# Priorities for the last exponentials and the merge, readings loaded one ahead, and the last store in halves, in an interleaved attention kernel

## The chip, the cores and the metric

The kernel runs on one core of a Trainium2 chip. A core has five engines that run side by side, each with its own queue of instructions: TensorE (PE in the profile, with its weight loads as PEld) multiplies matrices into PSUM; VectorE (DVE) and ScalarE (ACT) work on tiles element by element; GpSimd (POOL) works on tiles too; SyncE (SP) here only starts transfers. Transfers are also started from ScalarE's and GpSimd's queues. Engines wait for one another by semaphores, and an instruction that waits holds up all that stand behind it on its engine. The metric is the device time of one execution in microseconds (us).

## The reference

Four layers run one after the other on 2048 rows of 640 numbers, in the order A, B, A, B. Each adds its result to its input, after a layer norm without weights. Both have 32 heads of 20 numbers.

```python
def _A_ref(x, wqkv, wo):            # linear attention, not causal
    phi = lambda t: where(t > 0, t + 1, exp(t)) + 1e-6
    pq, pk = phi(q), phi(k)
    kv = einsum("bhsd,bhse->bhde", pk, v);  z = einsum("bhsd->bhd", pk)
    num = einsum("bhqd,bhde->bhqe", pq, kv)
    den = einsum("bhqd,bhd->bhq", pq, z)[..., None] + 1e-6
    return merge_heads(num / den) @ wo

def _B_ref(x, wq, wk, wv, wo, beta):  # 4 segments of 512 rows, with a memory M, z
    for s in range(4):
        p = softmax(qs @ ks.T * scale + causal_mask);  a_dot = p @ vs
        a_mem = (phi(qs) @ M) / (phi(qs) @ z + 1e-6)
        o = g * a_mem + (1 - g) * a_dot
        M, z = M + phi(ks).T @ vs, z + phi(ks).sum()
    return merge_heads(o) @ wo

x = A_x
for layer in (_A_ref, _B_ref, _A_ref, _B_ref):
    x = x + layer(layernorm(x), ...)
```

## The kernel before

The rows are cut into four segments of 512, and each segment into four tiles of 128 rows. Matrices that need more than 16 bits are kept as an upper half and a lower half (two f16 numbers whose sum is the value): ScalarE writes the upper half, VectorE subtracts it from the source and writes the lower half, and TensorE multiplies three of the four pairs. So a lower half on VectorE always stands behind an upper half on ScalarE. PSUM is used as a ring of eight banks, `ps`.

The order of TensorE's instructions is that in which the program issues them (`MANUAL = ("PE",)`). For the other engines a scheduler sets the order, by priority (by default the place in the program) and by what it thinks is ready; `high_priority(offset=...)` raises or lowers what is issued under it, and `issue_after(x)` keeps instructions behind x on their engine or by a wait.

**Layer A, first pass** (`g_first`). A tile x of 128 rows is loaded (L342, on SP's queue). `moments` takes its mean and variance on VectorE (L350 to L354) and the power -1/2 on GpSimd (L355); `shift` multiplies mean and scale into the bias `nb` (L360); `normed` writes the normalised tile xh on ScalarE (L386). `turn` transposes xh on TensorE (L331; three 128x128 blocks into one bank, two into another) and writes xT, the upper half on ScalarE (L335) and the lower on VectorE (L336). `proj_n` projects (L414). phi of keys and queries is an exponential and a relu on ScalarE (L428, L430) and a VectorE step (L431); the upper halves of the keys are L566 on ScalarE and the lower ones L553 on VectorE. `parts` copies xh for the product of keys and rows (L497 on ScalarE). `opening` weaves the first segment's norms, turns and weights together; there TensorE's order has the five transposes of tile 2 and the first three of tile 3 in one piece. Weights arrive as f32 in `stage` (L241), are scaled, split (L271 upper, L272 lower) and stored (L277, SP's queue).

**Merge.** At the end of the pass `merge` folds the sums G (L612 adds to them) and the values' and output's weights into one matrix wm per layer. For each half n it scales five parts (L669, L671), splits them (L673 upper, L674 lower), and TensorE multiplies them with w_Av (L692). The kt parts follow (L698, L701, L702), the products with the output weights (L722, L728), and the split of wm (L731 upper, L732 lower). In the first layer the last weight, w_Bo, is split at the same time: five L272 of 128x640 on VectorE. `open_b` then sets a tile `one` (L841, a memset on VectorE) and copies it into the key stacks (L844, six small transfers on SP's queue).

**Layer A, second pass** (`a_head`, `a_second`). `p_load` reads phi of the queries back from DRAM (L754, SP's queue); `p_read` scales it (L764), sums it per head (L768), takes the reciprocal (L769, L770) and multiplies (L771 on GpSimd). The result is turned (L331, L335, L336 into oT), multiplied by wm (L414) and added to the input xo (L342 for the load, L493 for the addition). `tail` turns the last two tiles of the segment for layer B, while TensorE has begun layer B's values.

**Layer B.** `b_project` projects values, which ScalarE spreads out with a column of ones per head (`v_half`, L445), then queries and keys (L399, split in L850 and L851, phi in L438 to L441). `attention` runs over 32 groups of four heads per layer. A group's stacks qs and ks are loaded; TensorE computes scores (L1015) of which VectorE takes row maxima (L1021, two instructions each, and L1030 and L1031 to split them); the maxima are turned (L1039) and stored as extra rows of qs; then the scores come again with the maximum in them (L1056), ScalarE takes exponentials (L1060), GpSimd zeroes what lies above the diagonal (L1067), and TensorE multiplies with the values (L1083). `EXPS` names the exponentials in five steps k. Steps 0 to 3 run in the group's own time slot, step 4 in the next one. `b_out` multiplies with w_Bo and adds the input (L490 and L491, or L493 at the very end, where the segment has `ends`), and stores the tile of 128x640 (L982, on ScalarE's queue).

## Time and profile before

| | us |
|---|---|
| median of 3 runs | 1696.86 (1695.87 to 1697.17) |
| the profiled execution's own time | 1699.81 |
| its span in the profile | 1698.1 |
| PE busy | 1641.3 |
| DVE busy | 1264.6 |
| ACT busy | 995.1 |
| POOL busy | 505.9 |

In rows of the waits, an engine and line stand before the arrow and the line that released it behind, then us in total, number of waits and the longest. In rows of a timeline stand the start, the duration, the engine, the line, the operation, `out<-in`, and in brackets the idle time ahead of it with its releaser; neighbouring equal instructions are one row (`x13`). In rows of stretches stand the stretch, its length, the busy us of PE, PEld, DVE, ACT and POOL with counts, the granted clock of TensorE (1.00 is full), and the share and GB/s of the DMA engines. Line numbers are those of the kernel before; those of the kernel after are a few higher.

### The profile page before, as it was taken

What the parts mean: (1) busy time and instruction counts of PE and PEld (TensorE: products, weight loads), DVE (VectorE), ACT (ScalarE), POOL (GpSimd) and SP (SyncE); (2) the same over time, 40 slices, a digit from 0 to 9 for tenths busy, and PEclk for the clock granted to TensorE, in tenths of its full rate; (3) what the DMA queues carried; (4) which work ended last, traced back from release to release, by engine and by line L of the source; (5) the groups of instructions that cost most, each with busy time, mean ns of one, the idle gap of its engine ahead of it and who ended that gap; (6) DMA issues with size and microseconds to landing.
All of it is one profiled execution on the core that took longest, in us unless ns stands there. A gap on an engine that the chain in (4) does not pass through costs nothing. (4 is left out here: it accounts for less than half of the span.)

```text
span 1698.1 us, 37894 instructions
## 1 busy us (share of the span) xinstructions
PE 1641.3 (97%) x13818; PEld 1021.1 (60%) x13818; DVE 1264.6 (74%) x4015; ACT 995.1 (59%) x1888; POOL 505.9 (30%) x1046
## 2 busy tenths in 40 slices
PE   8999989999999999999999999999999999999998
PEld 6767767564565566556556777766546546645555
DVE  7788886497887787768864566938888888777773
ACT  6666543357657656667665554433675675666763
POOL 4442232022223423433342211210322332232542
PEclk9999999999999999999999999999999999999999
DMA  6415563422312331461211303533232333323422
GB/s 219 156 57 184 214 246 119 148 87 78 114 68 70 127 111 60 134 206 51 80 45 48 108 32 124 191 97 119 76 111 82 104 100 102 106 83 111 148 87 95
DMA packets 110371, 190.99 MB, mean 112 GB/s; under 512 B 14172, under 2 KB 69596, under 8 KB 107624
## 3 DMA queue, kind: packets, MB, share of 16 engines
q1 hardware_dynamic: 97704, 142.68, 26.0%
q0 software_dynamic: 3264, 24.91, 4.1%
q10 hardware_dynamic: 9216, 20.98, 3.2%
q8 instruction: 109, 1.79, 0.4%
q14 instruction: 78, 0.64, 0.1%
HBM read 109.32 MB, written 78.64 MB: 111 GB/s over the span
## 5 line engine op out<-in xcount | busy, mean ns | idle before, releaser
L1021 DVE CUSTOM_DVE_ANT_0 ps<-ps,maskw 128x512 f32<-128x512 f32 (+3 forms) x1024 | 472.1, 521 | 43.8 <-PE ps L1015 41.6
L1060 ACT ACTIVATE pe<-ps,lsc 128x512 f32<-128x512 f32 x640 | 396.7, 696 | 84.5 <-PE ps L1056 82.7
L1067 POOL TENSOR_SCALAR_AFFINE_SELECT pe<-pe 128x256 f32<-128x256 f32 (+1 forms) x640 | 233.3, 372 | 387.6 <-ACT pe L1060 379.6
L414 PEld LDWEIGHTS <-xT 128*128 128x128 f16 x2880 | 280.3, 98 | 112.5 <-issue 6.2
L414 PEld LDWEIGHTS <-oT 128*128 128x128 f16 x1920 | 185.5, 98 | 82.3 <-issue 6.8
L1083 PE MATMUL ps<-pe,v 128*32 128x512 f32 (+3 forms) x2048 | 166.4, 436 | 7.8 <-POOL pe L1067 2.2
L414 PE MATMUL ps<-w_Bo,oT 128*128 128x320 f16 x960 | 143.5, 302 | 3.6 <-ACT oT L335 2.0
L1021 DVE DVE_READ_ACCUMULATOR2_ANT mg<- 128x1 f32 x1024 | 145.2, 142 | 0.0
L590 PE MATMUL ps<-pk,xs 128*128 128x321 f16 (+1 forms) x960 | 138.4, 302 | 4.2 <-DVE pk L553 2.0
L399 PE MATMUL ps<-xT,w_Bq 128*128 128x512 f16 x600 | 140.9, 380 | 1.3 <-ACT pe L1060 0.8
L414 PE MATMUL ps<-wm,oT 128*128 128x320 f16 x960 | 141.0, 299 | 0.5
L414 PE MATMUL ps<-w_Ak,xT 128*128 128x320 f16 x960 | 139.0, 300 | 2.3 <-DVE xT L336 1.6
L414 PE MATMUL ps<-w_Bv,xT 128*128 128x320 f16 x960 | 139.3, 299 | 1.9 <-ACT v L445 1.8
L399 PE MATMUL ps<-xT,w_Bk 128*128 128x512 f16 x600 | 138.5, 379 | 1.2 <-ACT pe L1060 1.2
L414 PE MATMUL ps<-w_Aq,xT 128*128 128x320 f16 x960 | 137.6, 299 | 0.0
L1015 PE MATMUL ps<-ks,qs 60*128 60x512 f16 (+3 forms) x1024 | 123.1, 298 | 8.5 <-DVE mg L1021 3.5
L590 PEld LDWEIGHTS <-xs 128*128 128x128 f16 x960 | 93.2, 98 | 43.6 <-DVE pk L553 2.6
L431 DVE SCALAR_TENSOR_TENSOR e<-e,r 128x320 f32<-128x320 f32 x128 | 67.9, 531 | 67.3 <-ACT r L430 66.9
L1083 PEld LDWEIGHTS ps<-pe,v 128*32 128x32 f32 x2048 | 64.7, 109 | 74.8 <-issue 45.0
L1056 PE MATMUL ps<-qs,ks 62*128 62x128 f16 (+3 forms) x1024 | 105.2, 300 | 1.1 <-ACT pe L1060 1.1
L851 DVE SCALAR_TENSOR_TENSOR nat<-ps,nat 128x512 f16<-128x512 f32 x80 | 55.2, 690 | 64.2 <-ACT nat L850 63.8
L399 PEld LDWEIGHTS <-w_Bk 128*128 128x128 f16 x600 | 57.0, 98 | 66.3 <-issue 6.2
(202 smaller groups left out, 2367.6 us busy)
## 6 DMA issues: line engine op xcount, KB each, us to landing
x<-xn ACTq DMA_DIRECT2D x48, 320.0 KB
qs<-qd SPq DMA_DIRECT2D x128, 120.0 KB
ks<-kd SPq DMA_DIRECT2D x128, 120.0 KB
xo<-x SPq DMA_DIRECT2D x48, 320.0 KB
pqi<-pqd SPq DMA_DIRECT2D x32, 320.0 KB
qd<-nat SPq DMA_DIRECT2D x40, 256.0 KB
kd<-nat SPq DMA_DIRECT2D x40, 256.0 KB
x<-in_A_x SPq DMA_DIRECT2D x16, 320.0 KB
```

The source lines that it names most:

```text
L399: nc.tensor.matmul(p, w[:, c, a, t * P:(t + 1) * P], xT[:, c, b, :], start=k == 0, stop=k == 3 * C - 1)
L414: nc.tensor.matmul(p, xT[:, c, a, i * P:(i + 1) * P], w[:, c, b, n * HN:(n + 1) * HN], start=k == 0, stop=k == 3 * C - 1)
L431: nc.vector.scalar_tensor_tensor(e, e, 1.0, r, op0=OP.min, op1=OP.add)
L590: nc.tensor.matmul(p, xs[:, i, a, c * P:(c + 1) * P], pk[i][:, b, cols], start=i == 0 and a == b, stop=i == NT - 1 and a == 1)
L851: nc.vector.scalar_tensor_tensor(nat[:, 1], p, QK_SHIFT, nat[:, 0], op0=OP.mult, op1=OP.subtract)
L1015: nc.tensor.matmul(bs[par][:, a:a + n], qs[r, p, i * P:(i + 1) * P], ks[r, p, :n], start=True, stop=True)
L1021: nc.vector.tensor_tensor_reduce(bs[par][:, a:a + n], bs[par][:, a:a + n], self.maskw[:, SEG - n:], 1.0, NEG, OP.add, OP.max, G["mg"][:, p ...
L1056: nc.tensor.matmul(b[:, a:a + n], ks[r, p, j * P:(j + 1) * P], qs[r, p, j * P:], start=True, stop=True)
L1060: nc.scalar.activation(e, b, AF.Exp, scale=self.lsc)
L1067: nc.gpsimd.affine_select(d, d, pattern=pat, compare_op=OP.is_ge, fill=0.0, base=0, channel_multiplier=-1)
L1083: nc.tensor.matmul(G["pv"][32 * h4:32 * h4 + 32, j * P:], v[j][:, h * E1:h * E1 + 32], G.pop((p, par, j)), start=j == 0, stop=j == 2, skip ...
```

## The change

It has these parts.

- In the opening, the shifts L360 of tiles 2 and 3 are no longer issued with their moments, but each just ahead of its own L386 and behind the lower halves of the tile before (`self.lower`).
- The five lower halves of w_Bo get a lower priority, and `open_b`'s memset and copies come behind the last lower half of kt (`L["split"]`).
- In `tail`, the shift and L386 of a segment's last tile come behind both parts of the turn before and behind the last spread of v (`self.spread`).
- In `a_head`, for segments 1 to 3, the reading of tile i + 1 is loaded ahead of the work on tile i. Which engine does the work is as before.
- The exponentials of step 4 get a higher priority.
- The last tile of the last segment is stored in two halves of columns, each behind its own addition.

```diff
@@ -269,8 +269,9 @@
         for cols in (slice(0, HN), slice(HN, D)) if key == ("A", "k") else (slice(0, D),):
             for c in range(C):
                 nc.scalar.activation(w[:, c, 0, cols], st[:, c, cols], AF.Copy, scale=scl)
-                self.last = nc.vector.scalar_tensor_tensor(w[:, c, 1, cols], st[:, c, cols], scl, w[:, c, 0, cols],
-                                                           op0=OP.mult, op1=OP.subtract)
+                with self.tc.high_priority(offset=-400) if key == ("B", "o") else nullcontext():
+                    self.last = nc.vector.scalar_tensor_tensor(w[:, c, 1, cols], st[:, c, cols], scl, w[:, c, 0, cols],
+                                                               op0=OP.mult, op1=OP.subtract)
                 if c < C - 1:
                     yield 0.0
         wd = self.dr.tile([P, C, 2, D], F16, name="wd_%s%s" % key)
@@ -442,8 +443,8 @@
 
     def v_half(self, p, v, n):
         vv = v[:, :H * E1].rearrange("p (h e) -> p h e", e=E1)
-        self.nc.scalar.activation(vv[:, n * HB:(n + 1) * HB, :DH],
-                                  p.rearrange("p (h e) -> p h e", e=DH), AF.Copy, scale=V_SHIFT)
+        self.spread = self.nc.scalar.activation(vv[:, n * HB:(n + 1) * HB, :DH],
+                                                p.rearrange("p (h e) -> p h e", e=DH), AF.Copy, scale=V_SHIFT)
 
     def new_v(self, user):
 
@@ -754,10 +755,10 @@
         self.q_pqi.dma_start(pq, L["pqd"][s][i])
         return pq
 
-    def p_read(self, L, s, i, o, pq=None):
+    def p_read(self, L, s, i, o, pq=None, eng=None):
 
         nc = self.nc
-        eng = nc.gpsimd
+        eng = eng or nc.gpsimd
         if pq is None:
             pq, eng = self.p_load(L, s, i), nc.vector
         with self.tc.issue_after(L["split"].ins):
@@ -778,10 +779,12 @@
         box.update(o=[], oT=[])
         while L["kt"] is None:
             yield 0.0
-        pq = L["pre"] if s == 0 else [None] * 3
+        pq = L["pre"] if s == 0 else [self.p_load(L, s, 0)]
         box["oT"].append(self.new_oT())
         for i in range(3):
-            yield from self.p_read(L, s, i, box["o"], pq[i])
+            if s > 0 and i < 2:
+                pq.append(self.p_load(L, s, i + 1))
+            yield from self.p_read(L, s, i, box["o"], pq[i], self.nc.vector if s > 0 else None)
         while L["wm"] is None:
             yield 0.0
         yield from self.turn(box["o"][0], box["oT"][0], 0)
@@ -821,17 +824,17 @@
         def tail():
             t = self.turn(xh[NT - 2], xT, NT - 2)
             yield next(t)
-            with self.tc.issue_after(self.lower.ins):
-                m2 = self.shift(*m)
-            xh.append(self.normed(*m2))
-            yield from t
+            cost = next(t)
+            with self.tc.issue_after(self.lower.ins), self.tc.issue_after(self.spread.ins):
+                xh.append(self.normed(*self.shift(*m)))
+            yield cost
             yield from self.turn(xh[NT - 1], xT, NT - 1)
         box["tail"] = tail()
 
 
-    def open_b(self):
+    def open_b(self, L):
         self.bp = self.ctx.enter_context(self.tc.tile_pool(name="attn", bufs=1))
-        with self.tc.high_priority():
+        with self.tc.high_priority(), self.tc.issue_after(L["split"].ins):
             self.open_stacks()
 
     def open_stacks(self):
@@ -977,9 +980,14 @@
             for n in range(2):
                 yield from (c for c in [next(t, None)] if c)
                 self.o_half(oT[i], wo, "B", x, xn, n, later=not st.get("ends"), begun=begun[n] if i == 0 else None)
+                split = st.get("ends") and i == NT - 1
+                if split:
+                    c = slice(n * HN, (n + 1) * HN)
+                    self.q_x.dma_start(dst[s * SEG + i * P:s * SEG + i * P + P, c], xn[:, c])
                 yield self.COST_N
             r = s * SEG + i * P
-            self.q_x.dma_start(dst[r:r + P], xn)
+            if not split:
+                self.q_x.dma_start(dst[r:r + P], xn)
             made.append(xn)
             if norm and i > 0:
                 with self.tc.issue_after(self.lower.ins):
@@ -1140,8 +1148,9 @@
                     elif op == "rows":
                         self.max_rows(G)
                     elif op == "exp":
-                        for bank in EXPS[k]:
-                            self.scores(G, bank)
+                        with self.tc.high_priority(offset=200) if k == 4 else nullcontext():
+                            for bank in EXPS[k]:
+                                self.scores(G, bank)
                     elif op == "sum":
                         self.weigh(G, k)
                     elif op == "copy":
@@ -1216,13 +1225,16 @@
         self.key_scale()
         m = [m]
         with self.tc.issue_after(self.last.ins):
-            m += [self.moments(x[i]) for i in range(2, NT)]
+            m += [self.moments(x[i], False) for i in range(2, NT)]
         top = self.power
 
         def others():
             xh = [first]
             yield from pause(3)
             for i in range(1, NT):
+                if i > 1:
+                    with self.tc.issue_after(self.lower.ins):
+                        m[i - 1] = self.shift(*m[i - 1])
                 xh.append(self.normed(*m[i - 1]))
                 yield from self.turn(xh[i], cur[1], i)
                 if i == 1:
@@ -1269,7 +1281,7 @@
         wA = {}
         wB = {"o": self.w["B", "o"]}
         stage_ctx.close()
-        self.open_b()
+        self.open_b(L)
         i = 0
         while i < n:
             last = i + 2 >= n
```

TensorE's instructions and their order are the same in both kernels. On ScalarE in the opening, before (xh of tiles 2 and 3 are the two L386 in one row; what follows belongs to the keys of tile 1 and the turns of tiles 2 and 3):

```order
L566 ACTIVATE pk<-e,k_scl 128x320 x2
L386 ACTIVATE xh<-x,nb,rs 128x640 x2
L428 ACTIVATE e<-ps,inv_Ak 128x320
L430 ACTIVATE r<-ps,inv_Ak 128x320
L335 ACTIVATE xT<-ps 128x3x128
L335 ACTIVATE xT<-ps 128x2x128
L566 ACTIVATE pk<-e,k_scl 128x320
L497 ACTIVATE xs<-xh 128x640
L335 ACTIVATE xT<-ps 128x3x128
```

After, with lines one higher:

```order
L567 ACTIVATE pk<-e,k_scl 128x320 x2
L387 ACTIVATE xh<-x,nb,rs 128x640
L429 ACTIVATE e<-ps,inv_Ak 128x320
L431 ACTIVATE r<-ps,inv_Ak 128x320
L336 ACTIVATE xT<-ps 128x3x128
L336 ACTIVATE xT<-ps 128x2x128
L567 ACTIVATE pk<-e,k_scl 128x320
L498 ACTIVATE xs<-xh 128x640
L387 ACTIVATE xh<-x,nb,rs 128x640
L336 ACTIVATE xT<-ps 128x3x128
```

The second xh went behind the exponential, relu, two turns' upper halves, the key's upper half and the copy xs. Its bias comes from VectorE, where it now stands behind both lower halves of tile 2.

On VectorE in the first merge, before, from the first half's parts on (w_Bo's lower halves are L272, the parts' lower halves L674, the memset L841):

```order
L272 SCALAR_TENSOR_TENSOR w_Bo<-stage,scl_Bo,w_Bo 128x640 x4
L674 TENSOR_TENSOR xT<-ge,xT 128x320 x2
L671 SCALAR_TENSOR_TENSOR ge<-v_83,eps,rz 128x320
L669 TENSOR_SCALAR eps<-v_84,k_scl 128x1
L669 TENSOR_SCALAR eps<-g_last,k_scl 128x1
L671 SCALAR_TENSOR_TENSOR ge<-v_84,eps,rz 128x320
L674 TENSOR_TENSOR xT<-ge,xT 128x320
L671 SCALAR_TENSOR_TENSOR ge<-g_last,eps,rz 128x320
L674 TENSOR_TENSOR xT<-ge,xT 128x320
L612 TENSOR_TENSOR v_81<-ps,v_81 128x320
L674 TENSOR_TENSOR xT<-ge,xT 128x320
L272 SCALAR_TENSOR_TENSOR w_Bo<-stage,scl_Bo,w_Bo 128x640
```

After, the same place (L675 is the parts' lower half):

```order
L672 SCALAR_TENSOR_TENSOR ge<-v_83,eps,rz 128x320
L672 SCALAR_TENSOR_TENSOR ge<-v_84,eps,rz 128x320
L670 TENSOR_SCALAR eps<-g_last,k_scl 128x1
L613 TENSOR_TENSOR v_81<-ps,v_81 128x320
L672 SCALAR_TENSOR_TENSOR ge<-g_last,eps,rz 128x320
L297 TENSOR_TENSOR ioB<-inv_Bv,inv_Bo 128x1
L613 TENSOR_TENSOR v_82<-ps,v_82 128x320
L675 TENSOR_TENSOR xT<-ge,xT 128x320 x5
```

And after, further on, where the lower halves of wm (L733) end and oT begins (L337):

```order
L273 SCALAR_TENSOR_TENSOR w_Bo<-stage,scl_Bo,w_Bo 128x640
L771 RECIPROCAL rca<-rca 128x32
L733 SCALAR_TENSOR_TENSOR wm<-ps,wm 128x320 x2
L273 SCALAR_TENSOR_TENSOR w_Bo<-stage,scl_Bo,w_Bo 128x640
L733 SCALAR_TENSOR_TENSOR wm<-ps,wm 128x320 x2
L273 SCALAR_TENSOR_TENSOR w_Bo<-stage,scl_Bo,w_Bo 128x640
L733 SCALAR_TENSOR_TENSOR wm<-ps,wm 128x320 x2
L273 SCALAR_TENSOR_TENSOR w_Bo<-stage,scl_Bo,w_Bo 128x640
L733 SCALAR_TENSOR_TENSOR wm<-ps,wm 128x320
L844 MEMSET one 2x1024
L733 SCALAR_TENSOR_TENSOR wm<-ps,wm 128x320
L337 TENSOR_TENSOR oT<-ps,oT 128x3x128
```

w_Bo's lower halves (L273) and the memset (L844) moved from among the parts to among the lower halves of wm; one of the five stands ahead of the last two parts of the second half.

On ScalarE in the tail of a segment of the first layer, before (L445 is the spread of v, L1060 the exponentials, L386 the xh of the segment's last tile):

```order
L445 ACTIVATE v_81<-ps 128x16x20
L1060 ACTIVATE pe<-ps,lsc 128x512 x4
L335 ACTIVATE xT<-ps 128x3x128
L386 ACTIVATE xh<-xn,nb,rs 128x640
L445 ACTIVATE v_81<-ps 128x16x20
L1060 ACTIVATE pe<-ps,lsc 128x512 x4
L335 ACTIVATE xT<-ps 128x2x128
L445 ACTIVATE v_82<-ps 128x16x20
```

After (the same lines are L446, L1068 and L387):

```order
L446 ACTIVATE v_81<-ps 128x16x20
L1068 ACTIVATE pe<-ps,lsc 128x512 x4
L336 ACTIVATE xT<-ps 128x3x128
L446 ACTIVATE v_81<-ps 128x16x20
L1068 ACTIVATE pe<-ps,lsc 128x512 x4
L336 ACTIVATE xT<-ps 128x2x128
L387 ACTIVATE xh<-xn,nb,rs 128x640
L1068 ACTIVATE pe<-ps,lsc 128x512 x2
```

The last xh went from ahead of the second spread to behind it, behind four exponentials and the second part of the turn.

## The prediction

> **What bounds the kernel now.** I read the page's busy times first, then what TensorE waited for, then the stretches in which its clock fell, and then the engines' timelines at those places. One execution is profiled; with what lies around its span it took 1699.81 us, 2.95 above the median of 1696.86. I work out a difference against the profiled execution and put it on the median.
>
> ```profile
> span 1698.1 us, 37894 instructions
> PE 1641.3 (97%) x13818; PEld 1021.1 (60%) x13818; DVE 1264.6 (74%) x4015; ACT 995.1 (59%) x1888; POOL 505.9 (30%) x1046
> ```
>
> TensorE is busy for all but 56.8 us, and its order of work is written out and the same in both kernels. So the change can only act by TensorE's short waits, by its clock, and by what follows its last matmul. The waits that the change can reach, as us in total, number, longest:
>
> ```profile
> PE ps L692 <- DVE xT L674: 2.3, 5, 0.6
> PE ps L1083 <- POOL pe L1067: 2.2, 7, 0.6
> PE ps L414 <- ACT v L445: 1.8, 2, 0.9
> PE ps L414 <- DVE xT L336: 1.6, 1, 1.6
> PE ps L692 <- ACT xT L673: 1.6, 3, 0.7
> PE pm L1039 <- ACT v L445: 1.2, 4, 0.3
> ```
>
> The view by stretches gives the clock (PEclk, after the busy times of PE, PEld, DVE, ACT and POOL):
>
> ```profile
> 20.40:23.86 3.46, 1.45 (x10) 0.86 (x11) 2.49 (x11) 3.23 (x7) 2.65 (x5) 1.00 1.12 381
> 23.86:27.27 3.41, 3.41 (x16) 2.70 (x15) 1.61 (x5) 2.29 (x6) 2.36 (x8) 0.50 0.59 210
> 238.90:242.30 3.40, 1.87 (x27) 1.32 (x25) 3.40 (x10) 1.92 (x4) 1.07 (x4) 1.00 0.81 339
> 242.30:245.70 3.40, 2.23 (x19) 1.86 (x19) 3.33 (x11) 2.52 (x7) 0.25 (x2) 0.50 0.82 253
> 245.70:249.10 3.40, 3.40 (x26) 2.92 (x25) 2.52 (x8) 0.54 (x2) 1.14 (x4) 0.50 0.95 388
> ```
>
> A stretch of 3.4 us in which TensorE worked 1.45, 1.87 or 2.23 us was followed by one at half clock. Such a stretch costs half of the work in it, so up to 1.7 us. These rows are the price of every new idle time below.
>
> **1. Opening: the shifts of tiles 2 and 3 come later.** Now:
>
> ```profile
> 22.86 2.72 PE L414 MATMUL ps<-w_Ak,xT 128*128 128x320 f16 x13 [1.63 <-DVE xT L336]
> 25.37 1.92 PE L331 MATMUL ps<-ident,xh 128*128 128x128 f32 x8
> 21.55 0.21 DVE L360 TENSOR_SCALAR nb<-mv,rs 128x1 f32<-128x1 f32 x1 [0.44 <-POOL rs L355]
> 27.00 0.88 DVE L336 TENSOR_TENSOR xT<-ps,xT 128x384 f16<-128x384 f32 x2
> 22.77 1.73 ACT L386 ACTIVATE xh<-x,nb,rs 128x640 f32<-128x640 f32 x2
> 25.61 0.53 ACT L428 ACTIVATE e<-ps,inv_Ak 128x320 f32<-128x320 f32 x1 [1.12 <-PE ps L414]
> 27.59 0.72 ACT L497 ACTIVATE xs<-xh 128x640 f16<-128x640 f32 x1
> 28.22 0.47 ACT L335 ACTIVATE xT<-ps 128x384 f16<-128x384 f32 x1
> ```
>
> VectorE's first L360 sat 0.44 us waiting for GpSimd in front of the L336 that TensorE waited for. Without it and its own 0.14 us, L336 ends 0.58 us earlier. TensorE restarts at 22.28 and, since more of its matmuls now fall before the half clock of 23.86, reaches the eight transposes at about 24.2 instead of 25.37: a gain of 1.1 at this point.
>
> It is lost at once. The eight transposes are five of tile 2 and three of tile 3, the sixth starting at about 26.5. Their inputs are the two L386 of the row at 22.77. The second now needs a shift that is issued behind both L336 of tile 2 (the row at 27.00), and on ScalarE it stands behind L428 to L497, where the row at 28.22 now follows. With that run 1.1 us earlier, L497 ends at 27.1, L386 takes 0.9, and TensorE gets tile 3 at 28.0 instead of 26.5. Then the stretch 23.86 to 27.27 holds only some 1.7 us of TensorE's work (23.86 to 25.6). By the rows above (1.45, 1.87 and 2.23 led to half clock), the next stretch, to 30.7, runs at half clock: from 28.0 to 30.7 that does 1.35 us of work, where before 0.4 (26.5 to 27.27 at half) and 3.4 were done. Loss 2.45. Without the clock's part it is 28.0 + 2.7 of work against the same 3.8, a loss of 1.1. Later waits may absorb some; I take +2.2, ends +0.5 and +3.3. [...]
>
> Four loads of weights also pass four loads of x on SP's queue. No wait on those x shows in this stretch, so I cost that at nothing; were the cover gone, the price would be that of a late L386, already in the upper end.
>
> **2. First merge: w_Bo's lower halves and the memset leave the front of VectorE.** Now:
>
> ```profile
> 228.91 3.26 DVE L272 SCALAR_TENSOR_TENSOR w_Bo<-stage,scl_Bo,w_Bo 128x640 f16<-128x640 f32 x4
> 236.13 0.88 DVE L272 SCALAR_TENSOR_TENSOR w_Bo<-stage,scl_Bo,w_Bo 128x640 f16<-128x640 f32 x1
> 237.63 0.91 DVE L841 MEMSET one<- 2x1024 f16 x1
> 258.83 1.35 DVE L336 TENSOR_TENSOR oT<-ps,oT 128x384 f16<-128x384 f32 x3
> 228.79:258.83 30.04, 25.81 (x226) 17.92 (x223) 26.98 (x68) 13.82 (x34) 7.89 (x16) 0.89 0.56 209
> 257.72 1.09 PE L331 MATMUL ps<-ident,pqi 128*128 128x128 f32 x8
> 258.85 2.53 PE L414 MATMUL ps<-wm,oT 128*128 128x320 f16 x15
> 238.57 4.52 SPq L844 DMA_DIRECT2D ks<-one  x6
> 261.76 0.54 DVE L493 SCALAR_TENSOR_TENSOR xn<-ps,ioG,xo 128x320 f32<-128x320 f32 x1
> ```
>
> Five L272 and a memset, 5.0 us, stood ahead of the L674 for which TensorE waited 2.3 + 1.6 = 3.9 us; the two half-clock stretches held 2.23 + 3.40 us, so cost 2.8. All of it goes: TensorE could begin the matmuls of the row at 258.85 some 6.7 us earlier, at 252.2. But the five L272 are not gone: one now sits among the last L674, four between the L732, the memset before the last L732. VectorE was busy 26.98 of the 30.04 us up to L336 of oT. It does the same work, so that L336 cannot start before 228.79 + 26.98 = 255.8. That is 3.06 us earlier, not 6.7. TensorE then idles from 252.2 to 255.8, almost a whole stretch of the clock's grid (252.5 to 255.9), and by the rows above the next runs at half clock: +1.7. Net -1.4, ends -4.5 (if VectorE's work packs tighter) and +1.0.
>
> On SP's queue the store of w_Bo, the six L844 and then the first xo load stand in this order. The memset ends near 255.3, the L844 take 4.52, so xo is issued near 260 and lands behind 1.6 MB, near 263.5; L493 now waits there instead of at 261.76, with the L336 of tile 2's oT behind it on VectorE. TensorE needs that near 267, so I cost it at nothing; each us that xo lands after 265.5 would cost a us.
>
> **3. The last tile's L386 goes behind the spread of v.**
>
> ```profile
> 363.39 0.92 ACT L386 ACTIVATE xh<-xn,nb,rs 128x640 f32<-128x640 f32 x1 [0.75 <-DVE nb L360]
> 364.22 0.42 ACT L445 ACTIVATE v<-ps 128x320 f32<-128x320 f32 x1
> 364.69 1.52 PE L414 MATMUL ps<-w_Bv,xT 128*128 128x320 f16 x10 [0.93 <-ACT v L445]
> ```
>
> L445 waited behind 0.92 us of L386, and TensorE for L445. Behind it, L445 starts 0.8 us earlier. The six such waits are the rows of 1.8 and 1.2: at most -3.0. The tile's transposes stand a v tile further on in TensorE's order, which is L386's cover. Part of what is won will meet the row maxima next; I take -2.2, ends -3.0 and -0.8.
>
> **4. Readings loaded one ahead.** Their VectorE work (L764, L768, L769, L770) now starts behind the last turn of the segment. The waits from 366 to 384 us:
>
> ```profile
> PE ps L1015 <- DVE mg L1021: 1.0, 2, 0.6
> PE ps L1083 <- DVE m L1031: 0.2, 1, 0.2
> ```
>
> ```profile
> L764 DVE TENSOR_TENSOR pqi<-pqi,z 128x640 f32<-128x640 f32 x26 | 23.6, 909 | 4.0 <-DMA pqi<-pqd 4.0
> ```
>
> The row maxima L1021 were late behind a reading's L764. The second layer has the same rows from 1195 to 1213; its last segment adds 0.5 (L1083 for L1067, the seventh wait of the row of 2.2): 2.9 in all. The work only moves to later row maxima, so I take -1.6, ends -2.9 and +1.5 (half of the 2.9 with its sign turned). The loads L754 pass the store of w_Bo in the merge and, in the last segment of the second layer, fall behind a group's stack loads. VectorE waited 4.0 us in the whole run for such loads, beside other work of TensorE, so loading one ahead gives nothing by itself.
>
> **5. Exponentials of step 4 ahead of phi.** ScalarE's order moves at about 17 of 64 groups. There lie the other six waits of L1083 for L1067, which follows L1060: four like the first of these rows (457 to 462 us), and the two of the second (777 to 906).
>
> ```profile
> PE ps L1083 <- POOL pe L1067: 0.2, 1, 0.2
> PE ps L1083 <- POOL pe L1067: 0.9, 2, 0.6
> ```
>
> That is 1.7. Phi's two activations then come late for their own readers, so I take a third, -0.6, ends -1.5 and +0.5.
>
> **6. Last store in halves.**
>
> ```profile
> 1694.35 0.55 DVE L493 SCALAR_TENSOR_TENSOR xn<-ps,ioB,xo 128x320 f32<-128x320 f32 x1 [1.49 <-PE ps L414]
> DMA  0000000000000029990000000000002999100000
> ```
>
> The DMA row cuts 1688 to 1698.1 into 40; the last 320 KB take some four parts of 0.25 us. Half of it, 0.5, is saved if transfer time rules, nothing if the rest is fixed: -0.4, ends -0.6 and 0.
>
> **Sum:** +2.2 - 1.4 - 2.2 - 1.6 - 0.6 - 0.4 = -4.0, so 1695.8 for the profiled execution and 1692.8 on the median, faster by 0.24%. About 0.2%, 3.4 us, is what a measurement of this kernel can tell from no change.
>
> **Rivals.**
> (a) Gains hold in full: the opening costs 0.5, the merge gives 3.0 because its new idle trips no half clock, steps 3 and 4 give 3.0 and 2.5, the rest 1.0. That is -9.0, 1687.9. For it: each wait named is directly behind the moved work. Against: the clock rows.
> (b) Given back: the waits of 3 and 4 turn into the next ones (-0.8, -0.5), the rest as forecast: +2.2 - 1.4 - 0.8 - 0.5 - 0.3 - 0.4 = -1.2, 1695.7. For it: VectorE is busy 74% of the span, and nearly always in the merge.
> (c) Slower: the moved readings land ahead of row maxima without slack. One reading is L764 and L768, 0.8 us each. If at each of the six segments 1.3 us of that reach TensorE, step 4 costs +7.8 instead of -1.6, and the sum is +5.4: 1702.3. It decides from 1.0 us a segment on, where the sum (-2.4 without step 4) passes +3.4. Against it: the work moved is the same in amount, and between the row maxima VectorE has idle time on average.
> (d) The priority does not do what it says, since ScalarE's order is unchanged at three quarters of the groups: step 5 gives 0, 1693.4; it lies within the forecast.
>
> **Chances.** Forecast with (d) 0.36, its own range 1690 to 1695.5; (a) 0.28; (b) 0.18; (c) 0.18. The forecast's own range reaches past 1693.5, so 0.10 of it counts as no change: faster 0.26 + 0.28 = 0.54, same 0.10 + 0.18 = 0.28, slower 0.18. The range 1686.5 to 1700 leaves out the best of (a), 0.07, and the worse part of (c), 0.12.
>
> **What the changed profile would show.** Right: a wait of TensorE of over 1 us for xh L386 near 26 us with a half-clock stretch after 27.3; no wait for xT L674, and one of 2 to 3.5 us for oT L336 or wm L732 near 253 with half clock after 255.9; no waits for v L445; fewer for mg L1021 near 370 and 1200; the end 0.4 us sooner after the last matmul. Wrong: no L386 wait at the opening, xo late by more than 2 us, or new mg waits from 380 to 415 and 1360 to 1385.

## The result

The changed kernel takes 1685.05 us (median of 4 runs, 1682.14 to 1685.65), the kernel before 1696.36 (1695.55 to 1697.17). The ratio is 0.993, with a 95% interval of 0.9918 to 0.9943: 9.7 to 13.9 us faster. The forecast was 4.0 us. The sign was right, but the time lies below the range. In what follows, one execution of one experiment, which took 4411 us, is left out.

The page's busy times, after, in a span of 1683.9 us:

```profile
PE 1629.4 (97%) x13818; PEld 1017.3 (60%) x13818; DVE 1259.5 (75%) x4015; ACT 994.3 (59%) x1888; POOL 503.9 (30%) x1046
```

The span fell by 14.2 us, PE's busy time by 11.9. TensorE does the same work, so most of what went was never shown as idle time of its matmuls. (Up to its last matmul, the profiled execution before has 20.5 us at half clock and the one after 17.1, which explains 1.7 us of it at most.) Since its order is the same in both kernels, the 13818 matmuls can be paired. The table has the start of some pairs in the two profiled executions, and the difference.

| matmul | before | after | difference |
|---|---|---|---|
| first L414 behind the opening's L336 | 22.86 | 21.97 | -0.9 |
| tile 3's first transpose | 26.44 | 27.77 | +1.3 |
| L414 a little later | 29.57 | 33.16 | +3.6 |
| merge, first L692 that waited | 233.99 | 236.97 | +3.0 |
| merge, in L722 | 249.20 | 245.74 | -3.5 |
| first L414 that needs oT | 259.45 | 259.22 | -0.2 |
| L331 of tile 3's oT | 270.57 | 275.52 | +4.9 |
| L414 that waited for L445 | 364.69 | 369.02 | +4.3 |
| end of the first segment's readings | 383.96 | 388.72 | +4.8 |
| an L1083 in the first layer B | 638.62 | 638.26 | -0.4 |
| one behind the layer's last segment | 904.49 | 899.78 | -4.7 |
| second layer, L414 that waited for L445 | 1193.43 | 1188.54 | -4.9 |
| an L1083 in its last segments | 1448.80 | 1438.39 | -10.4 |
| one near the end | 1671.19 | 1657.43 | -13.8 |
| end of the span | 1698.1 | 1683.9 | -14.2 |

So the opening and the merge lost 5 us, and the two layers B won 18. The waits after, of the matmuls (lines are a few higher: L415 was L414, L332 L331, L693 L692, L1091 L1083):

```profile
PE ps L415 <- DVE oT L337: 5.6, 3, 3.4
PE ps L332 <- ACT xh L387: 4.2, 4, 2.7
PE ps L1091 <- POOL pe L1075: 1.1, 2, 0.5
PE ps L693 <- DVE xT L675: 0.9, 1, 0.9
```

The forecast's new waits are there, and those for L445 are gone from the list. But this list is not where most of the gain was. The same view for the engine's weight loads, before:

```profile
PEld ps L1083 <- POOL pe L1067: 25.4, 69, 0.9
```

And after:

```profile
PEld ps L1091 <- POOL pe L1075: 14.4, 42, 0.9
```

The loads ahead of the products with the values waited 25.4 us for masked exponentials, where the matmuls themselves had shown 2.2. One place where the matmuls showed no wait at all shows how. Before:

```profile
482.39 0.69 ACT L1060 ACTIVATE pe<-ps,lsc 128x512 f32<-128x512 f32 x1 [2.85 <-PE ps L1056]
482.98 0.91 ACT L386 ACTIVATE xh<-xn,nb,rs 128x640 f32<-128x640 f32 x1
483.79 0.67 ACT L1060 ACTIVATE pe<-ps,lsc 128x512 f32<-128x512 f32 x1
483.55 2.13 PE L1083 MATMUL ps<-pe,v 128*32 128x384 f32 x24
485.05 0.15 PEld L1083 LDWEIGHTS ps<-pe,v 128*32 128x32 f32 x6 [0.47 <-POOL pe L1067]
```

And after:

```profile
485.75 1.26 ACT L1068 ACTIVATE pe<-ps,lsc 128x512 f32<-128x512 f32 x2 [2.85 <-PE ps L1064]
486.91 0.92 ACT L387 ACTIVATE xh<-xn,nb,rs 128x640 f32<-128x640 f32 x1
486.92 1.51 PE L1091 MATMUL ps<-pe,v 128*32 128x384 f32 x24
```

The same 24 matmuls take 2.13 us before and 1.51 after. Before, they are shown as one unbroken busy stretch, although the weight load in the middle of it waits 0.47 us. The second of the two exponentials stands behind L386, and GpSimd's mask (L1067) and the weight load wait for it. The first experiment moves these exponentials alone.

### The profile page after: what moved, and what is told of

Its sections match the earlier page's. It is cut to its first block, busy times and chain, and to the rows that moved or that the text cites. A ratio compares the mean times of both kernels' runs of the same rounds, so it can differ in the third digit from the quotient of the medians.

```text
span 1683.9 us, 37903 instructions
## 1 busy us (share of the span) xinstructions
PE 1629.4 (97%) x13818; PEld 1017.3 (60%) x13818; DVE 1259.5 (75%) x4015; ACT 994.3 (59%) x1888; POOL 503.9 (30%) x1046
## 4 chain that ended last, share of the span: by engine, by line
PE 73%; DVE 10%; ACT 8%; DMA 3%; issue 2%; SPq 1%; POOL 1%; ACTq 0%; DVEq 0%; POOLq 0%
PE ps L415 30%; PE ps L400 14%; PE ps L1091 8%; PE ps L591 4%; PE ps L1064 4%; PE ps L332 4%; ACT pe L1068 3%; PE ps L1023 3%; PE ps L468 2%; PE ps L1104 2%; DVE e L432 1%; DVE wmx L245 1%; DVE ps L1029 1%; ACT xh L387 1%; PE ps L881 1%
## 5 line engine op out<-in xcount | busy, mean ns | idle before, releaser
L1068 ACT ACTIVATE pe<-ps,lsc 128x512 f32<-128x512 f32 x640 | 394.4, 695 | 83.3 <-PE ps L1064 81.4
L415 PEld LDWEIGHTS <-xT 128*128 128x128 f16 x2880 | 281.0, 98 | 110.4 <-issue 4.1
L1075 POOL TENSOR_SCALAR_AFFINE_SELECT pe<-pe 128x256 f32<-128x256 f32 (+1 forms) x640 | 229.8, 366 | 376.8 <-ACT pe L1068 373.4
L415 PEld LDWEIGHTS <-oT 128*128 128x128 f16 x1920 | 186.4, 99 | 89.1 <-DVE oT L337 8.3
L1091 PE MATMUL ps<-pe,v 128*32 128x512 f32 (+3 forms) x2048 | 157.8, 436 | 6.8 <-ACT pe L1068 2.1
L415 PE MATMUL ps<-wm,oT 128*128 128x320 f16 x960 | 144.1, 303 | 5.8 <-DVE oT L337 5.4
L415 PE MATMUL ps<-w_Bo,oT 128*128 128x320 f16 x960 | 143.1, 301 | 3.6 <-ACT oT L336 2.0
L415 PE MATMUL ps<-w_Ak,xT 128*128 128x320 f16 x960 | 140.5, 302 | 1.6 <-DVE xT L337 1.0
L415 PE MATMUL ps<-w_Bv,xT 128*128 128x320 f16 x960 | 139.3, 299 | 0.1
L415 PE MATMUL ps<-w_Aq,xT 128*128 128x320 f16 x960 | 137.6, 299 | 0.0
L1091 PEld LDWEIGHTS ps<-pe,v 128*32 128x32 f32 x2048 | 63.5, 109 | 64.4 <-issue 45.8
L336 ACT ACTIVATE oT<-ps 128x384 f16<-128x384 f32 (+1 forms) x128 | 55.9, 445 | 72.3 <-PE ps L332 55.3
```

The costliest lines, as they stand in the source:

```text
L336: self.upper = nc.scalar.activation(hi, v, AF.Copy)
L415: nc.tensor.matmul(p, xT[:, c, a, i * P:(i + 1) * P], w[:, c, b, n * HN:(n + 1) * HN], start=k == 0, stop=k == 3 * C - 1)
L1068: nc.scalar.activation(e, b, AF.Exp, scale=self.lsc)
L1075: nc.gpsimd.affine_select(d, d, pattern=pat, compare_op=OP.is_ge, fill=0.0, base=0, channel_multiplier=-1)
L1091: nc.tensor.matmul(G["pv"][32 * h4:32 * h4 + 32, j * P:], v[j][:, h * E1:h * E1 + 32], G.pop((p, par, j)), start=j == 0, stop=j == 2, skip ...
```

## The experiments

Each experiment starts from the kernel before, unless it says otherwise. "Local" figures are taken from paired matmuls in the profiled executions.

**Step 4's exponentials alone.**

```diff
-                        for bank in EXPS[k]:
-                            self.scores(G, bank)
+                        with self.tc.high_priority(offset=200) if k == 4 else nullcontext():
+                            for bank in EXPS[k]:
+                                self.scores(G, bank)
```

> The kernel before with only the higher priority of step 4's exponentials. My theory after seeing the two traces: the price of a late exponential is not in the waits of TensorE's matmuls (2.2 us for L1067) but in the waits of the weight loads ahead of them (25.4 us for L1067 before, 14.4 after), so this part alone takes 7 to 11 us: 1685.5 to 1689.5 against 1696.4, and the weight loads' wait for L1067 falls from 25 to about 15 us. The rival is the size on record, 0.6 us, with the gain of the whole change coming from the tail's L386: 1695.8, and the weight loads' wait stays above 20 us.

1685.9 us (median of three) against 1695.9, ratio 0.9943 (0.9924 to 0.9963): 9.7 us faster. This one part carries most of the gain. A second execution of the same kernel gave a profile:

> Step 4's exponentials alone, once more, for a profile at the usual clock. My theory: the weight loads wait for L1067 some 16 to 19 us in about 50 waits, against 25.4 in 69 before, the steps near 459, 485, 613, 638, 793, 904, 1288, 1313, 1423 and 1448 us each give 0.6 to 1.1 us, and the time is near 1686. The rival: without the tail's part these steps are smaller than half of that.

It took 1685.6 us. The steps at 459.5, 485.0, 613.2, 638.6, 793.4, 904.5, 1288.1, 1313.6, 1423.3 and 1448.8 us are 0.78, 0.65, 0.82, 0.63, 0.93, 1.12, 0.79, 0.65, 0.81 and 0.65, 7.8 in all. At the place shown above, L386 now stands behind both exponentials and the 24 matmuls take 1.51 us:

```profile
481.45 1.26 ACT L1060 ACTIVATE pe<-ps,lsc 128x512 f32<-128x512 f32 x2 [2.85 <-PE ps L1056]
482.61 0.92 ACT L386 ACTIVATE xh<-xn,nb,rs 128x640 f32<-128x640 f32 x1
482.62 1.51 PE L1083 MATMUL ps<-pe,v 128*32 128x384 f32 x24
```

The weight loads' row over the whole run:

```profile
PEld ps L1083 <- POOL pe L1067: 15.4, 47, 0.9
```

It falls by 10.0 us, a little more than expected and about as much as the time. Both versions of the rival fall.

**The exponentials of all steps.** The same edit without `if k == 4`.

> The kernel before with the higher priority for the exponentials of all five steps, not of step 4 alone. If what counts is that any exponential stands behind phi on ScalarE, the weight loads' remaining 41 waits for L1067 (14.2 us with step 4's part in) fall further and this is 2 to 6 us faster than step 4's part alone: 1680 to 1684. The rival: steps 0 to 3 have the rest of their group's slot as cover, and phi and the spreads of v, put behind, hold TensorE up in their place: the same as step 4's part or slower, 1686 to 1692.

1687.1 us, ratio 0.9950 (0.9935 to 0.9966): not shown to differ from step 4 alone. Its waits, of the weight loads and of the matmuls:

```profile
PEld ps L1083 <- POOL pe L1067: 15.0, 45, 0.9
PE ps L1083 <- ACT r L440: 3.3, 6, 0.7
PE ps L414 <- ACT pe L1060: 3.1, 5, 1.2
```

Against this stands the row of the kernel before:

```profile
PE ps L1083 <- ACT r L440: 0.9, 3, 0.6
```

The other steps' waits for the mask don't fall further (15.0 against 15.4), and phi's relu now holds TensorE up by 3.3 us in place of 0.9. L414's waits for exponentials, 0.6 us in all before and with step 4 alone, are 3.1 here. The rival holds.

**The tail's L386 alone.**

```diff
-            with self.tc.issue_after(self.lower.ins):
-                m2 = self.shift(*m)
-            xh.append(self.normed(*m2))
-            yield from t
+            cost = next(t)
+            with self.tc.issue_after(self.lower.ins), self.tc.issue_after(self.spread.ins):
+                xh.append(self.normed(*self.shift(*m)))
+            yield cost
```

> The kernel before with only the last tile's L386 moved behind the spread of v. My theory: the six waits for L445 go, and with them the weight loads' waits for the exponentials that stand behind L445; aligned matmul by matmul, the whole change gains 1.0 at the two places of the first segments and 1.3 at the other four, 7.3 in all, so this part alone gives 5 to 7.5 us: 1689 to 1691.5. The rival is the size on record (2.2, at most 3.0): 1693.4 to 1694.2, with the steps near 502, 656, 1331 and 1466 us being those of step 4's exponentials.

1689.4 us, ratio 0.9961 (0.9948 to 0.9975): 6.6 us faster. Locally each of the two places behind the first segments gives 1.09 at the matmul that waited, of which 0.3 is left 20 us later. Each of the other four gives 1.3, in three steps of 0.49, 0.48 and 0.33: the wait of the matmul L1039, which the forecast counted, and two waits of weight loads, which it did not. At one of these places before, in the weight loads from 502 to 505 us:

```profile
PEld ps L1083 <- POOL pe L1067: 0.7, 2, 0.4
```

In this experiment the row is gone there, and over the run it is

```profile
PEld ps L1083 <- POOL pe L1067: 22.1, 58, 0.9
```

Against the paired matmuls, L445 starts 1.6 us sooner there, and the exponentials queued behind it 1.5. With 1.3 more near 1345 us these places make 7.1 us.

**The readings loaded one ahead, alone.**

```diff
-        pq = L["pre"] if s == 0 else [None] * 3
+        pq = L["pre"] if s == 0 else [self.p_load(L, s, 0)]
...
+            if s > 0 and i < 2:
+                pq.append(self.p_load(L, s, i + 1))
+            yield from self.p_read(L, s, i, box["o"], pq[i], self.nc.vector if s > 0 else None)
```

> The kernel before with only the readings loaded one ahead. My theory: nothing, since the gains near 378, 382, 1207, 1210 and 1347 us came with the tail's change alone (its run shows them), and VectorE does the same work in nearly the same place: 0.5 us faster to 1.0 slower, 1695.4 to 1696.9 against 1695.9. The rival is the size on record, 1.6 us faster: 1694.3.

1696.4 us against 1696.7, ratio 0.9996 (0.9982 to 1.0009): nothing. The steps that I had put down to it (1.6 together at 378 and 381.7 us, the same near 1207 and 1210, and 1.3 near 1345) are in the tail's experiment. Those near 380 and 1208 are given back there at once: from 383 to 384 us the paired matmuls lose 1.5 again.

**The opening's shifts alone.**

```diff
-            m += [self.moments(x[i]) for i in range(2, NT)]
+            m += [self.moments(x[i], False) for i in range(2, NT)]
...
+                if i > 1:
+                    with self.tc.issue_after(self.lower.ins):
+                        m[i - 1] = self.shift(*m[i - 1])
```

> The kernel before with only the two shifts of the opening deferred. My theory: TensorE waits about 2.7 us for xh of tile 3 and then runs at half clock, a loss of 3.3 us that nothing later absorbs: 1699.0 to 1700.0. The rival: it is absorbed later when nothing else is changed, 1696.0 to 1697.5.

1700.6 us, ratio 1.0029 (1.0018 to 1.0039): 4.9 us slower, more than expected. TensorE's timeline and two stretches:

```profile
27.61 0.91 PE L331 MATMUL ps<-ident,xh 128*128 128x128 f32 x3 [2.71 <-ACT xh L386]
23.50:26.98 3.48, 1.01 (x7) 0.53 (x5) 1.95 (x5) 3.48 (x8) 2.83 (x8) 1.00 0.88 325
26.98:30.39 3.41, 2.78 (x11) 1.85 (x12) 0.56 (x1) 1.07 (x2) 1.24 (x1) 0.50 1.04 408
```

The wait is 2.71 us long, and half clock follows a stretch with 1.01 us of work. In this execution that was one stretch; in the changed kernel's it was two:

```profile
23.27:26.69 3.42, 1.40 (x10) 0.76 (x8) 1.60 (x6) 3.37 (x7) 2.92 (x6) 1.00 0.93 312
26.69:30.10 3.41, 2.33 (x10) 1.58 (x11) 0.93 (x2) 1.51 (x3) 1.53 (x5) 0.50 1.04 408
30.10:33.50 3.40, 3.40 (x15) 2.15 (x14) 0.00 (x0) 0.79 (x2) 0.00 (x0) 0.50 0.53 203
```

**The merge's part alone.**

```diff
+                with self.tc.high_priority(offset=-400) if key == ("B", "o") else nullcontext():
+                    self.last = nc.vector.scalar_tensor_tensor(...)
...
-        with self.tc.high_priority():
+        with self.tc.high_priority(), self.tc.issue_after(L["split"].ins):
             self.open_stacks()
```

> The kernel before with only the lower priority of w_Bo's lower halves and the later memset. My theory: the parts' waits and two half-clock stretches go (about 7 us), but a wait of 3.4 us for oT L336 with a half-clock stretch comes, and then a second wait of about 2 us for oT L336 of tile 2, behind an xo that lands late, with another half-clock stretch: 1.0 to 2.5 us slower, 1697.4 to 1699. The rival is the term on record without the late xo: 1.4 us faster, 1695.0.

1696.1 us against 1695.9, ratio 0.9997 (0.9984 to 1.0010): neither number; no change. Locally, in its profiled execution, the paired matmuls win 1.1 from 230 to 271 us, where the changed kernel's lose 1.8. The mechanism is the same in both. In the changed kernel, TensorE, then VectorE, then SP's queue:

```profile
259.22 3.39 PE L415 MATMUL ps<-wm,oT 128*128 128x320 f16 x13 [3.39 <-DVE oT L337]
272.13 3.38 PE L415 MATMUL ps<-wm,oT 128*128 128x320 f16 x13 [2.05 <-DVE oT L337]
269.82 1.01 DVE L494 SCALAR_TENSOR_TENSOR xn<-ps,ioG,xo 128x320 f32<-128x320 f32 x2 [6.12 <-DMA xo<-in_A_x]
256.96 0.32 SPq L278 DMA_DIRECT2D wd_Bo<-w_Bo  x1
258.39 4.16 SPq L847 DMA_DIRECT2D ks<-one  x6
262.59 7.78 SPq L343 DMA_DIRECT2D xo<-in_A_x  x4
```

And its stretches, each wait followed by half clock:

```profile
255.39:258.80 3.41, 0.44 (x2) 0.10 (x2) 3.25 (x7) 0.60 (x2) 0.00 (x0) 1.00 0.77 270
258.80:262.21 3.41, 2.99 (x12) 1.73 (x13) 3.19 (x7) 0.00 (x0) 0.30 (x1) 0.50 0.95 244
269.04:272.45 3.41, 1.36 (x12) 0.89 (x10) 2.63 (x8) 0.38 (x1) 0.00 (x0) 1.00 0.71 226
272.45:275.86 3.41, 3.41 (x15) 2.17 (x14) 3.11 (x11) 1.30 (x2) 0.69 (x2) 0.50 0.65 245
```

The first wait is the one forecast (3.39 us; forecast 3.6), with its half clock. The second was priced at nothing: xo, issued at 262.59, was there at 269.8, VectorE stood 6.12 us in front of L494, and the L337 of tile 2 behind it came 2.05 us late. In the experiment alone the second wait was 0.64 us, without a half-clock stretch behind it.

**The merge's part without the store of w_Bo.** Nothing reads that copy.

```diff
-        wd = self.dr.tile([P, C, 2, D], F16, name="wd_%s%s" % key)
-        nc.sync.dma_start(wd, w)
-        self.wd[key] = wd
+        if key != ("B", "o"):
+            wd = self.dr.tile([P, C, 2, D], F16, name="wd_%s%s" % key)
+            nc.sync.dma_start(wd, w)
+            self.wd[key] = wd
```

> The merge's part alone, without the store of w_Bo to DRAM, which nothing reads. My theory: the second wait for oT (0.6 to 2.0 us, tile 2) comes from xo landing behind those 1.6 MB, so it goes with the store, together with a half-clock stretch in the runs that had one: 1 to 3 us faster than the part alone, 1693 to 1695; the first wait for oT of 3.4 us stays. The rival: the six copies behind the late memset hold up xo by themselves, and it stays at 1696.

1693.8 us against 1696.7, ratio 0.9989 (0.9977 to 1.0002). The gain over the part alone is within the intervals; locally it is 2.0 us won instead of 1.1. The trace shows the way:

```profile
234.97 0.33 SPq L344 DMA_DIRECT2D xo<-in_A_x  x1
252.27 4.29 SPq L846 DMA_DIRECT2D ks<-one  x6
256.72 6.59 SPq L344 DMA_DIRECT2D xo<-in_A_x  x3
255.92 0.55 DVE L495 SCALAR_TENSOR_TENSOR xn<-ps,ioG,xo 128x320 f32<-128x320 f32 x1 [0.66 <-PE ps L416]
```

The addition L495 now waits for TensorE and not for xo, and the second wait for oT is gone; the first, of 3.39 us, stays, as expected. But without the store the scheduler put the first xo load ahead of the six copies as well, at 234.97. So the late xo is the cause of the second wait, and whether the store or the copies made it late isn't told apart.

**w_Bo's lower halves on GpSimd.** In place of the lower priority, and with the memset on GpSimd and without the unread store:

```diff
+                    nc.gpsimd.tensor_scalar(st[:, c], st[:, c], scl, None, op0=OP.mult)
+                    self.last = nc.gpsimd.tensor_tensor(w[:, c, 1], st[:, c], w[:, c, 0], op=OP.subtract)
```

> Instead of a lower priority, w_Bo's lower halves are computed on GpSimd (two instructions each), the memset too, at its early place, and the unread store is left out. My theory: VectorE's 5 us are what bounds the merge, so without them on VectorE both the waits for the parts (3.8 us) and the wait for oT (3.4 us) stay away, and the half clock with them: 4 to 7 us faster, 1689 to 1692. The rival: GpSimd's 10 us or more delay its own L764 and L771 or slow VectorE beside it, and half or more of it is lost: 1693 to 1696.

1698.7 us, ratio 1.0015 (1.0003 to 1.0026): 2.5 us slower, outside both numbers. Groups of VectorE from 230 to 247 us, with GpSimd at work:

```profile
L679 DVE TENSOR_TENSOR xT<-ge,xT 128x320 f16<-128x320 f32 x10 | 7.6, 807 | 0.0
L617 DVE TENSOR_TENSOR v<-ps,v 128x320 f32<-128x320 f32 x3 | 1.4, 477 | 0.0
```

Before, the first of these (there L674) in the same stretch:

```profile
L674 DVE TENSOR_TENSOR xT<-ge,xT 128x320 f16<-128x320 f32 x10 | 4.6, 481 | 0.1
```

L674 went from a mean of 481 to one of 807 ns with GpSimd at work, while L617, which reads PSUM, took 477 against 478 before (there L612). The timeline of the two engines shows where the mean comes from:

```profile
229.72 4.65 POOL L273 TENSOR_SCALAR stage<-stage,scl_Bo 128x640 f32<-128x640 f32 x2
230.49 2.22 DVE L679 TENSOR_TENSOR xT<-ge,xT 128x320 f16<-128x320 f32 x5
234.35 3.01 POOL L274 TENSOR_TENSOR w_Bo<-stage,w_Bo 128x640 f16<-128x640 f32 x2
234.81 2.89 DVE L679 TENSOR_TENSOR xT<-ge,xT 128x320 f16<-128x320 f32 x2
```

Five of the ten fit into 2.22 us beside GpSimd's L273, and two beside its L274 took 2.89, the last ending 0.34 us after it. So taking work off VectorE slowed what was left on it: in these rows an L679 takes 0.4 us beside L273 and 1.4 beside L274. The one L617 beside L274, at 234.41, takes 0.48. Why L679 is slow there and L617 is not was not shown.

**The three gains together.** Step 4's exponentials, the tail's L386 and the store in halves:

> The kernel before with the three parts that the runs so far call gains: step 4's exponentials, the tail's L386, the last store in halves. If they are independent, 9.6 + 6.5 + 0.4 = 16.5 us come off: 1679.4 against 1695.9, and this beats the changed kernel by the 4.7 us of the opening and what the merge costs. The rival: they take the same waits twice (both move work in front of the exponentials on ScalarE), then 10 to 13 us: 1683 to 1686.

1680.7 us, ratio 0.9908 (0.9884 to 0.9933): 15.6 us faster, 11.4 to 19.7. The parts add up to 9.7 + 6.6, as measured, and the 0.4 of the store, which was not run alone: 16.7. So they are independent within what can be measured. The median is 4.4 us below the changed kernel's; the two ratios' intervals just overlap.

**A version that goes on from there.** The changed kernel without the readings loaded one ahead and without the unread store of w_Bo, and with another opening: both shifts and both L386 of tiles 2 and 3 are issued together, with high priority, behind tile 1's lower halves.

```diff
+                if i == 2:
+                    with self.tc.high_priority(), self.tc.issue_after(self.lower.ins):
+                        m[1:] = [self.shift(*a) for a in m[1:]]
+                        xh += [self.normed(*a) for a in m[1:]]
+                elif i == 1:
+                    xh.append(self.normed(*m[0]))
```

> A version for which the runs speak: step 4's exponentials, the tail's L386, the last store in halves, the merge's part without the unread store of w_Bo, and in the opening both shifts together directly behind tile 1's lower halves, with high priority, so that the two L386 stand side by side on ScalarE as before. My theory: 16.0 us from the three gains as measured together, 1 to 2.5 from the merge, 0.5 to 1.5 from the opening, since L336 no longer waits for GpSimd and tile 3 is in time: 1676.5 to 1680 against 1696.4, and the wait for xh near 26 us is gone. The rival: the opening's and merge's places still trip half clock and give nothing: 1680 to 1682.

1676.4 us (1675.9 to 1677.1), ratio 0.9886 (0.9871 to 0.9901): 20 us faster than before, 8.7 below the changed kernel's median. TensorE in the opening, and its longest wait of the whole run:

```profile
22.34 1.94 PE L416 MATMUL ps<-w_Ak,xT 128*128 128x320 f16 x13 [0.95 <-DVE xT L338]
24.12 1.04 PE L333 MATMUL ps<-ident,xh 128*128 128x128 f32 x8
PE ps L416 <- DVE oT L338: 3.6, 2, 3.4
```

The eight transposes run in one piece again, with L336's earlier end kept, and by 28 us of the run TensorE is 2.2 us ahead of the profile before. It was 0.2 behind at 20 us; 1.7 of the 2.4 are the half-clock stretch that this execution did not have there, since the tail's experiment, with the opening as it was and no such stretch, gains 1.7 too. The wait for oT in the merge is what is left there.

## Why the prediction was right or wrong

The sum was -4.0, the measured change -11.3 by the medians; the five parts that were run alone add up to -12.6. By term, with what the part did alone:

| step | on record | ends | alone |
|---|---|---|---|
| 1 opening | +2.2 | +0.5 to +3.3 | +4.9 (3.1 to 6.6) |
| 2 merge | -1.4 | -4.5 to +1.0 | -0.5 (-2.7 to +1.7) |
| 3 tail's L386 | -2.2 | -3.0 to -0.8 | -6.6 (-8.8 to -4.2) |
| 4 readings | -1.6 | -2.9 to +1.5 | -0.7 (-3.1 to +1.5) |
| 5 exponentials of step 4 | -0.6 | -1.5 to +0.5 | -9.7 (-12.9 to -6.3) |
| 6 store in halves | -0.4 | -0.6 to 0 | not run alone |

Step 5 failed first and most. It said that 1.7 us of matmul waits for L1067 lay at the places whose order moves, and took a third of it. The direction was right, and the six places that it named are six of the ten that gave the gain; at the other four (485.0, 638.6, 1313.6 and 1448.8 us) the matmuls show no wait before. The term was mis-sized by sixteen times, since it took the matmuls' list of waits for all of TensorE's waits. A wait of a weight load stands in another list and shows here as busy time in PE's rows (0.47 us of it in the 24 matmuls of 2.13). In that list stood 25.4 us for L1067, of which the part alone took 10.0.

Step 3 had the right mechanism and the right six places. Its end of -3.0 was the sum of the same list, and the 1.0 us that each of four places gave beyond its 0.3 are mostly weight loads, behind exponentials that were behind L445. The discount for waits that take their place was right in kind: 0.8 of each 1.09 behind the first segments was lost again. The 1.3 near 1345 us it did not name at all.

Step 1 forecast the wait for tile 3's xh (1.5 us beyond the old start; 1.3 measured) and the half clock behind it. The part alone lost 4.9 us, above the end of 3.3. Its mechanism was right, but the size was taken against a profile that had a half-clock stretch of its own at this place (from 23.86 us). Against that profile the paired matmuls of the opening's experiment lose 2.5 from 20 to 35 us, as the step worked out. Against the tail's experiment, which has the opening of before without such a stretch, they lose 4.2. The changed kernel's execution had a second half-clock stretch as well: the clock fell behind a stretch with 1.40 us of work and stayed down behind the next, which held 2.33.

Step 2 was right in the first wait and its half clock, though one wait of 0.9 us for a part's lower half (L693 for L675) was left where it had named none. It failed in "TensorE needs that near 267, so I cost it at nothing". xo was issued at 262.6, not near 260, and landed at 269.8, not near 263.5, 7 us after its issue behind a store of 1.6 MB. An xo late by more than 2 us was a sign of being wrong that the prediction named. By the price that the same step named, a us for each us after 265.5, that is 4.3; the wait was 2.05 and the half-clock stretch behind it 1.7, 3.75 together. That the first idle time fell almost whole into one window of the clock was partly chance: the step put it on the grid of the execution before (252.5 to 255.9), and in the changed kernel's execution it lay some 3.5 us later, on another grid (255.39 to 258.80). The grid is that of the traces: half-clock stretches begin at 23.86, 112.61, 242.31 and 1638.36 us before and at 26.69, 258.80, 272.45 and 1627.54 after, each 3.413 us times a whole number from the one ahead of it (26, 38 and 409; 68, 4 and 397).

Step 4 said 1.6 and was nothing: the waits it listed move with the tail's part, not with the loads, and the larger ones give nothing on balance. Step 6 is seen in the trace. The last addition before starts at 1694.35, with 3.75 us to the end of the span; after:

```profile
1680.59 0.55 DVE L494 SCALAR_TENSOR_TENSOR xn<-ps,ioB,xo 128x320 f32<-128x320 f32 x1 [1.49 <-PE ps L415]
```

From there it is 3.3 us, 0.45 less.

Of the rivals, (a), that the gains hold in full, came nearest with 1687.9. That is luck: steps 3 and 5 gave more than it had, and its opening, merge and readings did not come true. (b), (c) and (d) fell: most of what steps 3 and 5 won was kept, no row maximum became late by 1 us a segment, and the priority, though it moved a quarter of the groups, was the largest gain of all.

## What to carry to other kernels

Read the waits of the weight loads beside those of the matmuls, and compare the length of equal rows of matmuls: 24 of them at 2.13 us in one place and 1.51 in another, at the same granted clock (1.00 in both), are a wait, though the row says busy. A job of 0.9 us that nothing needs at once, on a shared engine, can cost most of its length wherever something short that TensorE needs stands behind it (here 0.6 us). Moving only the last step's exponentials was worth 10 us, and moving those of all steps added nothing that could be measured. When work moves out of a crowded stretch, follow the queues behind it (here a store of 1.6 MB and six small copies ahead of a load) to the instruction that waits in front of something else.

## What was not expected of the hardware

The half-clock stretches do not belong to fixed places of the kernel. The profiled execution before had one after the opening's idle time (stretch from 23.86). The experiment on the merge has the same opening, with the same idle time, and its clock stayed full there:

```profile
20.00:23.40 3.40, 1.48 (x10) 0.89 (x11) 2.43 (x11) 3.16 (x7) 2.69 (x5) 1.00 1.07 361
23.40:26.80 3.40, 3.40 (x29) 2.71 (x28) 2.38 (x6) 3.05 (x7) 3.04 (x8) 1.00 0.63 217
```

The first row is laid where the idle time is, not where this execution's clock has its windows. Its half-clock stretches in the merge begin at 250.11; counted back from there in steps of 3.413 us, the length of such a stretch in the trace, two windows share the idle time:

```profile
18.00:21.42 3.42, 2.08 (x13) 0.94 (x11) 2.98 (x12) 3.38 (x8) 1.11 (x2) 1.00 0.65 269
21.42:24.83 3.41, 2.46 (x20) 2.01 (x21) 2.35 (x7) 2.83 (x6) 3.00 (x6) 1.00 0.95 306
```

Neither holds as little as the 1.45 us of the execution before. Of nine profiles in which this opening is unchanged, four have a half-clock stretch that begins between 22 and 24 us, and five have none. A limit of work in a window does not come out of the traces, even on each one's own grid: a window with 1.76 us was followed by full clock (after, 115.44 to 118.85), and one with 2.45 by half (before, 1634.94 to 1638.36). So the rows of 1.45, 1.87 and 2.23 that the prediction priced by are cases and not a rule.

In 23 runs of the kernel before, on one chip, the time went from 1691.5 to 1701.1. Nor do the windows stand at the same place in each execution: they end at 23.86 us in the one before and at 21.42 and 24.83 in the experiment on the merge. So a stretch of 1.7 us lost in one profile is a chance, not a price, until several runs show it. That the spread of the runs comes from this alone was not shown.
